# Building three small constant tables on chip instead of loading them, in a chunked state-space scan followed by a bilinear feed-forward layer

## The chip, the cores and the metric

The kernel runs on one core of a Trainium2 chip. The core has a matrix engine (TensorE, PE in the profile), a vector engine (VectorE, DVE), a scalar engine (ScalarE, ACT), a general engine (GpSimd, POOL) and a queue engine (SyncE, SP). Loads and stores are issued from the SP, ACT and POOL queues and are carried out by 16 DMA engines. The metric is the device time of one execution in microseconds (us), as a median of several runs; lower is better.

## The reference, cut to what matters

There are 4 batches, 8 heads, 768 tokens, head width D = 32 and state width N = 16. The first half is a chunked scan with a decaying state, the second a bilinear feed-forward layer on the 3072 x 256 result with 1536 hidden columns.

```python
for c in range(nc):                                   # chunks of the sequence
    cum = np.cumsum(la, axis=-1)                      # la: log of the decays a
    L = np.exp(cum[:, :, :, None] - cum[:, :, None, :]) * causal
    y_intra = np.einsum('bhij,bhjd->bhid', np.einsum('bhin,bhjn->bhij', Cc, Bc) * L, xc)
    y_inter = np.einsum('bhin,bhnd->bhid', Cc, state) * np.exp(cum)[:, :, :, None]
    y[:, :, sl] = y_intra + y_inter
    decay_full = np.exp(np.sum(la, axis=-1))
    Bx = np.einsum('bhjn,bhjd->bhjnd', Bc, xc) * np.exp(cum[:, :, -1:] - cum)[:, :, :, None, None]
    state = decay_full[:, :, None, None] * state + np.sum(Bx, axis=2)
# ... y of all heads side by side: x of 3072 x 256
out = (x @ w_a * (x @ w_b)) @ w_out
```

## The kernel before

The sequence is cut into NBLK = 6 blocks of Q = 128 tokens. Two batches of a block make a *pair* (p = 0 to 11), the unit of all loads of B, C and x (`load1`, `load2`). For each pair, `scale_bc` multiplies B and C by decay factors, `transposes` turns them for TensorE, `scores` forms C times B for each head, `mask(product(...))` multiplies the scores by a causal mask, and `pv` multiplies them by x and adds what the state of the block before gives. The result, X2T, goes through the feed-forward layer in units (`unit`, `unit_mm`): products with w_a and w_b, a copy of the first out of PSUM on ScalarE (`evac_a`), the product of the two on VectorE (`times`), and products with w_out (`out_mm`).

The order of work is written out by hand: each engine runs its instructions in the order of the program, so on each queue an instruction waits behind everything that stands ahead of it. Idle stretches of TensorE near the start are filled by `warmup` products of a tile of zeros, whose results are not used.

What matters here is the front of the program:

- SP's and ACT's queues issue a (the decays) and the B, C and x of pair 0. SP's also loads two constant tables: `ch` (128 x 10, line 188) and `c32` (32 x 148, line 194). `ch` holds `headm` (which head a row of a 128-row head-by-state tile belongs to) and `par` (whether that head is even or odd). `c32` holds `indm` (32 x 128, which head a column belongs to) and `selb` (which batch a row belongs to).
- GpSimd makes `sel` (32 x 32, a selector of batch and head, lines 197 and 198), then the identity `ident` (lines 207 and 208), then the mask `causal` (lines 211 and 214), and then issues seven loads: the rest of pair 1's B and C, the first halves of the weights Wa and Wb (`load_w(0)`, line 171), and pair 1's x in two halves (`xn`).
- VectorE clears `warm` and `zero`, waits for a and runs the decay products (`scan`, line 233); then `sel_over_mid` (line 239) forms `selr` out of `sel`, and `factors_mm` (line 254) turns decays into factors with small fp32 products.
- `ident` is used by `transposes`, `par` by the ACT copies in `transposes` (line 345) and by `state_spread` (line 596), and `headm` by `maskbd` (line 825).
- The decay of the state over a whole block, `hs` (32 rows of batch and head x 5 blocks), is needed on 128 rows of head and state as `G`. Before the change GpSimd first spreads `hs` to 32 x 20 (`hsx`, line 797), zero outside a row's own batch, and one fp32 product with `indm` gives all of `G` (line 815). ScalarE's queue then holds, in this order, the copy of the factors (`fC`, line 267), the copy of `G` (line 817) and the scaling of pair 1's x (`scale_x(1, nc.scalar)`, line 291), which `pv(1)` waits for (line 448).

Of the kernel before, what the change touches and what calls it, by code (L numbers as in the profile page):

```python
# [10 lines left out]
f32 = mybir.dt.float32  # L11
# [3 lines left out]
ALU = mybir.AluOpType  # L15
# [13 lines left out]
def kernel(  # L29
# [13 lines left out]
    nc = tc.nc  # L43

    nb, H, S, D = x.shape
    N = B.shape[-1]
# [6 lines left out]
    BH = nb * H  # L53
    NBP = nb // 2
    NP = NBP * NBLK
    NG = NBLK - 1
# [1 line left out]
    P2 = 6  # L58


    j = np.arange(128)
    bh = np.arange(BH)
    p32 = np.zeros((BH, 128 + nb * NG), np.float32)
    p32[:, 0:128] = (bh[:, None] % H) == (j[None, :] // N)
    for b in range(nb):
        p32[b * H : (b + 1) * H, 128 + b * NG : 128 + (b + 1) * NG] = 1.0
    p32_t = nc.inline_tensor(p32, "p32")
    ph = np.zeros((128, H + 2), np.float32)
    ph[:, 0:H] = (j[:, None] // N) == np.arange(H)[None, :]
    ph[:, H:] = (j[:, None] // N) % 2 == np.arange(2)[None, :]  # L70
    ph_t = nc.inline_tensor(ph, "ph")

    const = ctx.enter_context(tc.tile_pool(name="const", bufs=1))
    c32 = const.tile([BH, p32.shape[1]], f32, name="c32")
    ch = const.tile([128, H + 2], f32, name="ch")
    ident = const.tile([128, 128], f16, name="ident")
    causal = const.tile([128, 2, Q], f16, name="causal")
    sel = const.tile([BH, 2, NBP, H], f32, name="sel")
    indm = c32[:, 0:128]
    selb = c32[:, 128 : 128 + nb * NG]  # L80
    headm = ch[:, 0:H]
    par = ch[:, H:]

    big = ctx.enter_context(tc.tile_pool(name="big", bufs=1))
    a_sb = big.tile([BH, NBLK, Q], f32, name="a_sb")
# [22 lines left out]
    fCl = big.tile([128, NL, NBP * 2 * H], f32, name="fCl")  # L108
    hr = big.tile([BH, NG], f32, name="hr")
    hs = big.tile([BH, NG], f32, name="hs")  # L110
    hsx = big.tile([BH, nb, NG], f32, name="hsx")
    G = big.tile([128, nb, NG], f32, name="G")

    inp = ctx.enter_context(tc.tile_pool(name="inp", bufs=3))
# [31 lines left out]
    def load1(eng, p, which, bt, i0=0, n=64):  # L146
        blk, bp = divmod(p, NBP)
        if p >= P2:
            return eng.dma_start(
                by_token(pair_in[p][which])[:, bt],  # L150
                (B, C, x)[which][2 * bp + bt, :, blk * Q : (blk + 1) * Q, :].rearrange("h q n -> q h n"),
            )
        src = (B, C, x)[which][2 * bp + bt, :, blk * Q + 2 * i0 : blk * Q + 2 * i0 + 2 * n, :]
        return eng.dma_start(  # L154
            pair_in[p][which][64 * bt + i0 : 64 * bt + i0 + n].rearrange("i h r n -> i h (r n)"),
            src.rearrange("h (i r) n -> i h (r n)", r=2),
        )
# [24 lines left out]
    for p_ in range(3):  # L182
# [2 lines left out]
    load1(nc.sync, 0, 0, 0)  # L185
    load1(nc.scalar, 0, 1, 1)
    load1(nc.sync, 0, 1, 0, 0, 32)
    nc.sync.dma_start(ch, ph_t.ap())
    load1(nc.scalar, 0, 1, 0, 32, 32)
    nc.scalar.preload_act_table_set("natural_log_exp_and_others")  # L190
    load1(nc.scalar, 0, 2, 1)
    load1(nc.sync, 0, 2, 0)
    load1(nc.sync, 1, 0, 0)
    nc.sync.dma_start(c32, p32_t.ap())
    nc.vector.memset(warm.bitcast(u32), 0)
    nc.vector.memset(zero, 0.0)
    nc.gpsimd.memset(sel, 1.0)
    nc.gpsimd.affine_select(
        out=sel,
        in_=sel,  # L200
        compare_op=ALU.is_equal,
        fill=0.0,
        base=0,
        pattern=[[-H, 2], [-2 * H, NBP], [-1, H]],
        channel_multiplier=1,
    )
    nc.gpsimd.memset(ident, 1.0)
    nc.gpsimd.affine_select(
        out=ident, in_=ident, compare_op=ALU.is_equal, fill=0.0, base=0, pattern=[[-1, 128]], channel_multiplier=1
    )  # L210
    nc.gpsimd.memset(causal, 1.0)
    for bt in range(2):
        v = causal[64 * bt : 64 * bt + 64]
        nc.gpsimd.affine_select(  # L214
            out=v, in_=v, compare_op=ALU.is_ge, fill=0.0, base=0, pattern=[[-1, 2], [1, Q]], channel_multiplier=-2
# [49 lines left out]
    def factors(lo, hi, fps):  # L265
        factors_mm(lo, hi, fps)
        nc.scalar.copy(flat(fC, lo, hi), fps[:, 0 : (hi - lo) * 2 * NBP * H])
# [56 lines left out]
    def transposes(p, ps=None, between=None, apart=False):  # L324
        s = st[p]
        if ps is None:
            ps = [SC[0], SC[1]] if apart else None
            on_dve = apart
        else:
            on_dve = True  # L330
        TB, TC = (TT[:, 0:256], TT[:, 256:512]) if ps is None else [t_.bitcast(f16)[:, 0:256] for t_ in ps]
        for T_, src in ((TB, s["bm"]), (TC, s["cm"])):
            for r in range(2):
                nc.tensor.transpose(
                    T_[:, r * 128 : (r + 1) * 128], src[:, r].rearrange("p h n -> p (h n)"), ident
                )
            if between:
                between()
                between = None
        BT = mid.tile([128, 2, 2, 2, 64], f16, name="bt", tag="bt")  # L340
        CT = mid.tile([128, 2, Q], f16, name="ct", tag="ct")
        b_ = []
        for e in range(2):
            o_ = BT[:, e].rearrange("p r t i -> p (r t i)")
            b_.append(nc.scalar.activation(out=o_, in_=TB, func=AF.Copy, scale=par[:, e : e + 1]))
        c_ = (nc.vector.tensor_copy if on_dve else nc.scalar.copy)(
            CT.rearrange("p t (i r) -> p r (t i)", r=2), TC.rearrange("p (r c) -> p r c", r=2)
        )
        if apart:
            for i_ in b_:  # L350
                tc.declare_no_dep(c_.ins, i_.ins.name, reason="reads of two banks")
        s["BT"], s["CT"] = BT, CT
# [288 lines left out]
    def unit(p, k2, between=None):  # L641
        a_ps = unit_mm(p, k2, Wa)
        if between:
            between()
        b_ps = unit_mm(p, k2, Wb)
        asb = evac_a(a_ps)
        return lambda: times(p, k2, b_ps, asb)
# [138 lines left out]
    for bt in range(2):  # L786
# [7 lines left out]
    sel_over_mid(1, P2 // NBP, nc.vector)  # L794
    nc.gpsimd.tensor_tensor(out=hr, in0=Pr[:, 0:NG, Q - 1], in1=rmid[:, 0:NG], op=ALU.mult)
    nc.gpsimd.tensor_tensor(out=hs, in0=hr, in1=Pr[:, 1:NBLK, 63], op=ALU.mult)
    nc.gpsimd.tensor_tensor(
        out=hsx,
        in0=hs.unsqueeze(1).broadcast_to((BH, nb, NG)),
        in1=selb.rearrange("p (b g) -> p b g", b=nb),  # L800
        op=ALU.mult,
    )
    for bt in range(2):
        load1(nc.gpsimd, 2, 0, bt)
    warmup(2, tcp)
# [6 lines left out]
    asb.append(evac_a(aps[2]))  # L812
    fps = bank("fps")
    gps = fps[:, 96 : 96 + nb * NG]
    nc.tensor.matmul(gps, indm, hsx.rearrange("p b g -> p (b g)"), start=True, stop=True, skip_group_check=True)
    factors(1, P2 // NBP, fps)
    nc.scalar.copy(G.rearrange("p b g -> p (b g)"), gps)
    scale_x(1, nc.scalar)
# [36 lines left out]
    h = unit(1, 5)  # L855
# [20 lines left out]
    h = unit(2, 0, lambda: transposes(3, apart=True))  # L876
# [3 lines left out]
    h = unit(2, 1)  # L880
# [55 lines left out]
    for m in range(1, 4):  # L936
# [36 lines left out]
        out=causal_q, in_=causal_q, compare_op=ALU.is_ge, fill=0.0, base=0, pattern=[[1, Q]], channel_multiplier=-1  # L973
# [97 lines left out]
```

## Time and profile before

| what | before |
|---|---|
| device time, median of 3 runs | 125.04 us |
| device time, lowest and highest | 124.65 and 125.16 us |
| span of the profiled execution, first to last instruction | 123.5 us |
| TensorE / VectorE / ScalarE / GpSimd busy | 95% / 70% / 58% / 51% |
| granted TensorE clock | full speed throughout |
| packets that the DMA engines moved | 60754, 13.74 MB |

The span is what the trace can explain; the median of the runs lies 1.5 us above it, which is what lies around the first and the last instruction. Busy shares are averages over the whole span. A line of a timeline reads: start in us from the span's start, length in us, engine, line of the kernel, operation, what is written and read, how many, and in square brackets how long the engine had been idle and what ended that. The ends of matrix products are modelled: two of them that follow each other overlap in the rows, and the distance of their starts is what the engine spends on one.

### The profile page before, as it was taken

Reading aid. Unit: us, or ns where it says so; the run is one execution under the profiler, and the core shown is the slowest. Engines: PE = TensorE matmul, PEld = TensorE weight load, DVE = VectorE, ACT = ScalarE, POOL = GpSimd, SP = SyncE. Lnnn points to the kernel's source line nnn. Section 1 sums busy time; section 2 is a strip of 40 time slices with the busy share of each in tenths; the row PEclk is TensorE's granted clock in tenths of the full one; section 3 lists DMA queues with packets and bytes.
Section 4 is the critical chain, followed back from the end, with each engine's and each line's share of the span. In section 5 each row is a group of like instructions: output and inputs, shape, how many; then the busy total and the mean of one; then the engine's idle time right before and its main releaser. Section 6 shows DMA issues by size and latency. Waiting matters only on the chain.

```text
span 123.5 us, 3874 instructions
## 1 busy us (share of the span) xinstructions
PE 117.6 (95%) x1527; PEld 79.8 (65%) x1527; DVE 86.4 (70%) x166; ACT 71.9 (58%) x142; POOL 62.8 (51%) x109
## 2 busy tenths in 40 slices
PE   5988999999999999899999999999999999999990
PEld 2445698978898788644467455756464784655880
DVE  1886889795968979298984989857899444847100
ACT  0465845866364795687758746664737736566220
POOL 7999999956873399089850895026900000000000
PEclk9999999999999999999999999999999999999999
DMA  3999999994659988697995973999541012010132
GB/s 64 154 163 237 171 196 181 194 145 74 99 115 185 92 83 147 84 120 79 134 155 74 150 264 87 70 95 161 113 130 42 5 42 85 0 42 0 48 101 69
DMA packets 60754, 13.74 MB, mean 111 GB/s; under 512 B 55632, under 2 KB 60400, under 8 KB 60736
## 3 DMA queue, kind: packets, MB, share of 16 engines
q1 hardware_dynamic: 56608, 9.53, 49.8%
q0 software_dynamic: 2128, 3.61, 16.3%
q10 hardware_dynamic: 2000, 0.36, 1.6%
q8 instruction: 12, 0.20, 0.7%
q14 instruction: 6, 0.05, 0.1%
HBM read 11.13 MB, written 3.15 MB: 116 GB/s over the span
## 4 chain that ended last, share of the span: by engine, by line
PE 83%; DMA 6%; POOL 5%; ACT 2%; issue 1%; DVE 1%; ACTq 0%; POOLq 0%
PE ops L709 18%; PE aps L682 17%; PE bps L682 17%; PE ops L652 9%; PE aps L616 8%; PE bps L616 7%; DMA xn<-in_x_dram 6%; PE SC L373 2%; PE SC L448 1%; PE SC L433 1%; PE SC L388 1%; POOL cn L154 1%; PE SC L523 1%; PE SC L475 1%; POOL bn L154 1%; POOL causal L214 1%
## 5 line engine op out<-in xcount | busy, mean ns | idle before, releaser
L630 ACT COPY asb<-aps 128x512 f32<-128x512 f32 x72 | 41.9, 587 | 14.8 <-PE aps L682 9.7
L694 DVE TENSOR_TENSOR hkb<-bps,asb 128x512 f16<-128x512 f32 x48 | 32.3, 689 | 12.9 <-ACT asb L630 11.7
L682 PE MATMUL aps<-XB,Wa 128*128 128x512 f16 x96 | 28.6, 379 | 0.0
L682 PE MATMUL bps<-XB,Wb 128*128 128x512 f16 x96 | 28.5, 379 | 0.0
L709 PE MATMUL ops<-Wo,hkb 128*128 128x256 f16 (+1 forms) x204 | 22.5, 267 | 0.0
L709 PEld LDWEIGHTS <-hkb 128*128 128x128 f16 x204 | 18.5, 98 | 3.1
L637 DVE TENSOR_TENSOR hk<-bps,asb 128x512 f16<-128x512 f32 x24 | 16.2, 688 | 2.9 <-ACT asb L630 2.4
L682 PEld LDWEIGHTS <-Wb 128*128 128x128 f16 x96 | 9.9, 103 | 11.0 <-issue 0.2
L427 DVE TENSOR_TENSOR t<-SC,causal_q 128x512 f16<-128x512 f32 x21 | 13.4, 682 | 3.9 <-PE SC L373 3.9
L682 PEld LDWEIGHTS <-Wa 128*128 128x128 f16 x96 | 9.7, 103 | 9.1 <-issue 0.4
L616 PE MATMUL aps<-X2T,Wa 128*128 128x256 f16 x96 | 14.3, 273 | 0.4 <-DMA Wa<-in_moe_w_a_dram 0.3
L721 ACT ACTIVATE osb<-ops 128x256 f32<-128x256 f32 (+1 forms) x16 | 6.0, 377 | 14.3 <-PE ops L709 14.2
L616 PE MATMUL bps<-X2T,Wb 128*128 128x256 f16 x96 | 14.3, 273 | 0.0
L652 PE MATMUL ops<-Wo,hk 128*128 128x256 f16 x96 | 11.6, 273 | 0.0
L616 PEld LDWEIGHTS <-Wa 128*128 128x128 f16 x96 | 9.5, 103 | 2.0 <-DMA Wa<-in_moe_w_a_dram 0.8
L616 PEld LDWEIGHTS <-Wb 128*128 128x128 f16 x96 | 9.7, 103 | 0.7
L652 PEld LDWEIGHTS <-hk 128*128 128x128 f16 x96 | 8.9, 98 | 1.5 <-DVE hk L637 0.2
L293 POOL TENSOR_SCALAR x<-xn 128x512 f16<-128x512 f32 x6 | 9.0, 1493 | 1.7 <-DMA xn<-in_x_dram 1.3
L427 DVE TENSOR_TENSOR t<-SC,causal 128x512 f16<-128x512 f32 x13 | 8.2, 684 | 1.4 <-PE SC L388 1.3
L304 POOL TENSOR_TENSOR planes<-cn,fCl 128x256 f16<-128x256 f32 x6 | 3.7, 622 | 8.1 <-DMA cn<-in_C_dram 8.1
L425 POOL TENSOR_TENSOR t<-tmp,causal_q 128x512 f16<-128x512 f32 x3 | 3.5, 1159 | 7.3 <-ACT tmp L424 7.2
L553 ACT ACTIVATE XB<-SC 64x512 f16<-64x512 f32 (+1 forms) x9 | 5.3, 594 | 2.9 <-PE SC L462 1.6
(102 smaller groups left out, 128.8 us busy)
## 6 DMA issues: line engine op xcount, KB each, us to landing
out_dram<-osb SPq DMA_DIRECT2D x19, 128.0 KB, 1.8
xn<-in_x_dram SPq DMA_DIRECT2D x5, 256.0 KB, 5.3
xn<-in_x_dram SPq DMA_DIRECT2D x7, 128.0 KB, 3.4
Wa<-in_moe_w_a_dram POOLq DMA_DIRECT2D x2, 384.0 KB, 6.2
Wb<-in_moe_w_b_dram POOLq DMA_DIRECT2D x2, 384.0 KB, 7.8
Wo<-in_moe_w_out_dram POOLq DMA_DIRECT2D x2, 384.0 KB, 6.8
cn<-in_C_dram SPq DMA_DIRECT2D x6, 128.0 KB, 4.2
bn<-in_B_dram SPq DMA_DIRECT2D x6, 128.0 KB, 4.3
```

Source lines behind the costliest of these rows:

```text
L293: eng.tensor_scalar(xo, xi, XS, None, ALU.mult)
L304: eng.tensor_tensor(out=planes[p % 2][:, 4:6].rearrange("p t (h n) -> p t h n", n=N), in0=raw, in1=f.unsqueeze(3).broadcast_to((128, 2, H, ...
L427: nc.vector.tensor_tensor(out=o_, in0=i_, in1=c_, op=ALU.mult)
L553: nc.scalar.activation(out=XB[to, blk - P0 // NBP, :, bt].rearrange("p u j q -> p u (j q)"), in_=SCt[bt][fr, :, 0 : NBP * Q], func=AF.Copy ...
L616: nc.tensor.matmul(ps[:, kk * 2 * Q : (kk + 1) * 2 * Q], W[k // 6][:, f, k % 6 // 3 * 384 : (k % 6 // 3 + 1) * 384].rearrange("p (c kk) -> ...
L630: (nc.vector.tensor_copy if on_dve else nc.scalar.copy)(asb, a_ps)
L637: nc.vector.tensor_tensor(out=s["hk"][:, 2 * k2 : 2 * k2 + 2, :].rearrange("p k q -> p (k q)"), in0=b_ps, in1=asb, op=ALU.mult)
L652: nc.tensor.matmul(o_ps[:, 0:d_model], hk[:, k, bt * Q : (bt + 1) * Q], Wo[:, k, :], start=(k == 0), stop=(k == NK - 1), skip_group_check= ...
L682: nc.tensor.matmul(t_, W[k // 6][:, f, k % 6 // 3 * 384 : (k % 6 // 3 + 1) * 384].rearrange("p (c kk) -> p kk c", kk=3)[:, k % 3], XB[:, b ...
L694: return lambda: nc.vector.tensor_tensor(out=s["hk"][:, k], in0=ps[1], in1=asb, op=ALU.mult)
L709: nc.tensor.matmul(o_ps[:, 0:w], hk[:, k, c * Q : (c + 1) * Q], Wo[:, k, cs], start=(k == 0), stop=(k == NK - 1), skip_group_check=True,)
L721: nc.scalar.activation(out=o_sb[:, 0:w], in_=o_ps[:, 0:w], func=AF.Copy, scale=1.0 / (YS * YS))
```

## The change

The tables `ch` and `c32` and their two loads go. VectorE makes `sel`, `headm`, `par` and a new table `spread` (32 x 32 x 16) from the identity, between its two clears and its first scan: two copies and two sums. GpSimd no longer makes `sel`, and starts with the identity. `hsx` goes as well: `G` comes out of four products, one for each batch, whose weights are the part of `spread` that holds that batch's eight heads, and whose moving tile is `hs` itself. The order of all other instructions on all engines stays as it was.

```diff
-    j = np.arange(128)
-    bh = np.arange(BH)
-    p32 = np.zeros((BH, 128 + nb * NG), np.float32)
-    p32[:, 0:128] = (bh[:, None] % H) == (j[None, :] // N)
...
-    ph_t = nc.inline_tensor(ph, "ph")
...
-    c32 = const.tile([BH, p32.shape[1]], f32, name="c32")
-    ch = const.tile([128, H + 2], f32, name="ch")
+    headm = const.tile([128, H], f32, name="headm")
+    par = const.tile([128, 2], f32, name="par")
...
+    spread = const.tile([BH, BH, N], f32, name="spread")
...
-    nc.sync.dma_start(ch, ph_t.ap())
...
-    nc.sync.dma_start(c32, p32_t.ap())
     nc.vector.memset(warm.bitcast(u32), 0)
     nc.vector.memset(zero, 0.0)
-    nc.gpsimd.memset(sel, 1.0)
-    nc.gpsimd.affine_select(
-        out=sel,
...
     nc.gpsimd.memset(ident, 1.0)
     nc.gpsimd.affine_select(
         out=ident, in_=ident, compare_op=ALU.is_equal, fill=0.0, base=0, pattern=[[-1, 128]], channel_multiplier=1
     )
+    nc.vector.tensor_copy(
+        sel.rearrange("p t b h -> p b t h"),
+        ident[0:BH, 0:BH].rearrange("p (b t h) -> p b t h", b=NBP, t=2),
+    )
+    nc.vector.tensor_reduce(
+        headm, ident.rearrange("p (h n) -> p h n", n=N), axis=mybir.AxisListType.X, op=ALU.add
+    )
+    nc.vector.tensor_reduce(
+        par, headm.rearrange("p (m e) -> p e m", e=2), axis=mybir.AxisListType.X, op=ALU.add
+    )
+    nc.vector.tensor_copy(spread, ident[0:BH, 0:BH].unsqueeze(2).broadcast_to((BH, BH, N)))
...
-    nc.gpsimd.tensor_tensor(
-        out=hsx,
-        in0=hs.unsqueeze(1).broadcast_to((BH, nb, NG)),
-        in1=selb.rearrange("p (b g) -> p b g", b=nb),
-        op=ALU.mult,
-    )
...
     gps = fps[:, 96 : 96 + nb * NG]
-    nc.tensor.matmul(gps, indm, hsx.rearrange("p b g -> p (b g)"), start=True, stop=True, skip_group_check=True)
+    for b in range(nb):
+        nc.tensor.matmul(
+            gps[:, b * NG : (b + 1) * NG],
+            spread[:, b * H : (b + 1) * H].rearrange("p h n -> p (h n)"),
+            hs,
+            start=True,
+            stop=True,
+            skip_group_check=True,
+        )
```

More of the change, by code (lines that the diff above doesn't have):

```diff
@@ L58 @@
     P2 = 6
-    j = np.arange(128)
-    bh = np.arange(BH)
-    p32 = np.zeros((BH, 128 + nb * NG), np.float32)
-    p32[:, 0:128] = (bh[:, None] % H) == (j[None, :] // N)
[L65 to L70, printed above, removed]
-    ph_t = nc.inline_tensor(ph, "ph")
     const = ctx.enter_context(tc.tile_pool(name="const", bufs=1))
-    c32 = const.tile([BH, p32.shape[1]], f32, name="c32")
-    ch = const.tile([128, H + 2], f32, name="ch")
+    headm = const.tile([128, H], f32, name="headm")
+    par = const.tile([128, 2], f32, name="par")
     ident = const.tile([128, 128], f16, name="ident")
@@ L78 @@
     sel = const.tile([BH, 2, NBP, H], f32, name="sel")
[L79 to L82, printed above, removed]
+    spread = const.tile([BH, BH, N], f32, name="spread")
     big = ctx.enter_context(tc.tile_pool(name="big", bufs=1))
@@ L110 @@
     hs = big.tile([BH, NG], f32, name="hs")
-    hsx = big.tile([BH, nb, NG], f32, name="hsx")
     G = big.tile([128, nb, NG], f32, name="G")
@@ L193 @@
     load1(nc.sync, 1, 0, 0)
-    nc.sync.dma_start(c32, p32_t.ap())
     nc.vector.memset(warm.bitcast(u32), 0)
     nc.vector.memset(zero, 0.0)
-    nc.gpsimd.memset(sel, 1.0)
-    nc.gpsimd.affine_select(
-        out=sel,
[L200 to L205, printed above, removed]
-    )
     nc.gpsimd.memset(ident, 1.0)
@@ L796 @@
     nc.gpsimd.tensor_tensor(out=hs, in0=hr, in1=Pr[:, 1:NBLK, 63], op=ALU.mult)
-    nc.gpsimd.tensor_tensor(
-        out=hsx,
-        in0=hs.unsqueeze(1).broadcast_to((BH, nb, NG)),
-        in1=selb.rearrange("p (b g) -> p b g", b=nb),
-        op=ALU.mult,
-    )
     for bt in range(2):
```

## The prediction

> **What bounds the kernel now.** I read the page first: engine shares and the chain that ended last.
>
> ```profile
> PE 117.6 (95%) x1527; PEld 79.8 (65%) x1527; DVE 86.4 (70%) x166; ACT 71.9 (58%) x142; POOL 62.8 (51%) x109
> ...
> PE 83%; DMA 6%; POOL 5%; ACT 2%; issue 1%; DVE 1%; ACTq 0%; POOLq 0%
> ```
>
> TensorE carries the chain. GpSimd and one DMA hold 11% of it, some 14 us, and the chain in order of time says where: all of it at the front.
>
> ```profile
> 0.79 0.12 POOL sel L197
> ...
> 0.98 0.25 POOL sel L198
> ...
> 2.94 0.84 POOL bn L154
> ...
> 6.60 0.65 POOL xn L154
> 7.25 7.34 DMA xn<-in_x_dram
> ...
> 14.67 0.64 ACT x L291
> ...
> 15.36 0.42 PE SC L448 x32
> ```
>
> GpSimd's table work and load issues run up to the load of pair 1's x, which lands at 14.59; ScalarE scales it and `pv(1)` starts at 15.36. After that the chain is TensorE almost without a break, so a shift of `pv(1)` is carried to the end. The case is decided by what sets 15.36. The timeline around it:
>
> ```profile
> 10.37 0.59 PE L226 MATMUL tc<-warm 128*128 128x512 f16 x2
> ...
> 11.23 0.78 PEld L616 LDWEIGHTS <-Wa 128*128 128x128 f16 x8 [0.76 <-DMA Wa<-in_moe_w_a_dram]
> ...
> 13.13 0.29 PEld L815 LDWEIGHTS fps<-hsx,c 32*128 32x128 f32 x2 [0.21 <-issue]
> 13.13 0.39 PE L815 MATMUL fps<-hsx,c 32*128 32x20 f32 x2
> ...
> 14.22 0.24 ACT L267 COPY fC<-fps 128x64 f32<-128x64 f32 x1
> 14.32 0.22 ACT L817 COPY G<-fps 128x20 f32<-128x20 f32 x1
> 14.67 0.63 ACT L291 ACTIVATE x<-xn 128x512 f16<-128x512 f32 x1
> ...
> 19.78 0.64 POOL L312 TENSOR_TENSOR bm<-bn,fB 128x256 f16<-128x256 f32 x1
> ```
>
> A second chain runs beside the first, and the chain of waits does not print it: Wa lands (11.23), TensorE goes on without idling to the product for G and the factors, ScalarE's copies wait for them, and `scale_x(1)` stands behind those copies. fC lasts 0.24 and G begins 0.14 before its end, so ScalarE could take the scaling at about 14.54 - 0.12 = 14.42. This chain has 0.25 us to spare against 14.67.
>
> The front, where the new work goes:
>
> ```profile
> 1.15 0.17 DVE L196 MEMSET zero<- 32x128 f32 x1
> ...
> 1.45 0.29 POOL L208 TENSOR_SCALAR_AFFINE_SELECT ident<-ident 128x128 f16<-128x128 f16 x1
> ...
> 3.06 0.41 DVE L233 TENSOR_TENSOR_SCAN Pr<-a_sb,zero 32x128 f32<-32x128 f32 x1 [1.74 <-DMA a_sb<-in_a_dram]
> ...
> 9.19 0.41 DVE L312 TENSOR_TENSOR cm<-cn,fC 128x256 f16<-128x256 f32 x1
> 9.23 0.85 POOL L312 TENSOR_TENSOR bm<-bn,fB 128x256 f16<-128x256 f32 x1
> ```
>
> VectorE sits idle for 1.74 us before its first scan, waiting for a. The busy table by half microseconds has the DMA share second from the end:
>
> ```profile
> 5.00:5.50 0.50, 0.50 (x3) 0.13 (x1) 0.47 (x2) 0.00 (x0) 0.50 (x2) 1.00 0.52 116
> 5.50:6.00 0.50, 0.38 (x5) 0.18 (x4) 0.44 (x2) 0.01 (x1) 0.50 (x2) 1.00 1.07 245
> ```
>
> The DMA engines are half free until 5.5 and, but for short dips, full after that.
>
> **The change part by part.** *GpSimd's two `sel` instructions go.* `sel` begins at 0.79 and the identity's clear at 1.19, so all that GpSimd does up to the issue of x moves up by 0.40 us: the identity is done at 1.34 instead of 1.74, the first load is issued at about 2.5 and not 2.9.
>
> *VectorE makes the tables.* Its four instructions wait for the identity, from about 1.40. The copy for `sel` is 32 elements deep: 0.17, as the clear of `zero`. The sum over 128 elements lies between that 0.17 and the 0.42 of a product over 256: 0.30. The sum for `par` waits for `headm` (0.10, as from `rmid` to `selr`) and costs 0.15, as the reciprocal of `rmid`. The copy for `spread` writes 512 elements: 0.27 (the clear of `warm`, 256 words) to 0.69 (a product over 512); I take 0.69. Sum 1.41, end 2.81, under the wait for a that ends at 3.06. So they cost nothing, with 0.25 us of cover; what they are late beyond it, the first scan and all of pair 0 are late. `selr`, the next reader, comes at 3.76.
>
> *Two loads leave SP's queue.* The load of `ch` takes SP 0.49 us (2.70 to the next issue at 3.19), that of `c32` 0.33. Pair 0's x is issued 0.4 to 0.5 sooner, and pair 1's B after it. Worth nothing by itself: the scaling of pair 0's x (7.85) stands behind ScalarE's copy at 7.37. Nothing waited for these tables: `ch` landed 2.7 after its issue, at 5.4, and its first use begins at 5.99.
>
> *The loads land sooner.* With issues 0.40 sooner Wa lands at 10.83 in place of 11.23. TensorE is free at 10.79 (its two warm-up products begin 0.21 apart: 10.37 + 0.42). So 0.40 us gained for the second chain; bounds 0 (the DMA engines are full, the data come no sooner) and 0.44 (TensorE itself is late next). I take 0.40, because the half-free stretch up to 5.5 can take the sooner packets. x lands at 14.19.
>
> *`hsx` goes.* GpSimd gets 0.27 us (12.18 to 12.44), behind which stand pair 2's loads and a mask; neither is on the path. `hs` is ready at 12.10 and its product comes at 12.73 at the soonest, so the product does not wait.
>
> *Four products for one.* Each fp32 product is two passes (L815 x2), so two passes become eight. Two weight loads of 0.182 take 0.29 together, so a further pass costs 0.11, and the moving width, 20 before and 5 after, hardly matters beside that. Six passes more: 0.65 us on TensorE. Bounds: 0.35 (the factor products, half as wide, have a pair of passes each 0.058) and 1.09 (no overlap of loads at all). I take 0.65: it is the same shape. Nothing hides it: the factor products stand behind it, then fC, G and the scaling of x.
>
> *The sum.* The second chain moves by +0.65 - 0.40, less its 0.25 to spare: the scaling of x starts at 14.67 as before, `pv(1)` at 15.36. The long wait for x (ends at 14.19 now) becomes a wait for the copies of the factors. Net 0.00: span 123.5, and with the 1.5 us by which the median lies above that span, 125.0 us.
>
> **The rivals.** *The passes are cheap.* At the lower bound of 0.35 the scaling starts at 14.67 + 0.35 - 0.65 = 14.37, and the landed x allows 14.27. Gain 0.30, 124.7 us. For it: narrow products do run closer together. Against it: the weights are 128 wide as before.
>
> *The loads are issued sooner but land no sooner.* Then the change does not do what it says: the 0.40 is missing and `pv(1)` is 0.40 late, 125.4 us. For it: DMA shares at or over 1 from 5.5 on. Against it: 0.52 just before. The Trainium skill ("DMA: Bandwidth & Descriptors", section "Issuing engines are not separate DMA queues") says that loads from all queues interleave on the same 16 engines and that several issuers save only issue time; by that rule this rival's 125.4 would be the time. The trace agrees as far as the full shares go, not in the half-free stretch.
>
> *VectorE's copies and GpSimd get in each other's way.* GpSimd's `bm` took 0.85 at 9.23, beside a VectorE product with both inputs in SBUF, and 0.64 at 19.78. If the copy for `spread` must wait until GpSimd's last select for `causal` ends (2.94 before, 2.54 now), it ends at 2.54 + 0.10 + 0.69 = 3.33. If in turn GpSimd's first load must wait for that, its issues are 0.44 later than before (3.33 against 2.89) in place of 0.40 sooner. Then Wa is 0.44 late and `pv(1)` 0.65 + 0.44 - 0.25 = 0.84: 125.9 us, slower by 0.7%. It decides the sign once GpSimd's first load is issued over 0.62 us later than at 2.5 (Wa is then 0.22 late, and 0.65 + 0.22 - 0.25 = 0.62). Against it: the copy may run in 0.3, and it may find a gap. The Trainium skill ("SBUF — State Buffer", section "Who interferes with whom") has such a rule: GpSimd and a VectorE copy in its two-port mode exclude each other for a whole instruction, sums never do; by it something between 125.4 and 125.9 would result. The stretch at 9.23 fits its further clause on VectorE instructions with two SBUF inputs; no VectorE copy out of SBUF is in the front of this trace.
>
> **How the numbers follow.** The forecast (125.0, within 0.2 of it by an uncertain 0.2 in the landing of Wa): 0.52. Cheap passes, 124.7: 0.14. No sooner landing, 125.4: 0.18. The mutual block, 125.9: 0.11. Unseen: 0.05. The range 124.5 to 125.6 takes in the first three, with 0.2 at the lower end for the scatter of the runs (124.65 to 125.16) and 0.2 at the upper. Half a per cent, 0.62 us, is about what a measurement of this kernel can tell from no change. Faster by more than that needs 0.3 more than the cheap passes give, and the landing of x allows 0.40 at most (14.27 against 14.67): 0.05, the unseen. Slower by more: the block and a little of the third case, 0.12. Within: 0.83.
>
> **What would show it.** Right: identity done near 1.34; VectorE's tables done before 3.06 and the first scan there still; Wa's wait over near 10.8; eight passes on the four products (line 793 of the changed kernel) 0.11 apart, 0.9 us in all; the scaling of x waiting for TensorE's factors and no longer for the DMA; `pv(1)` within 0.2 of 15.36. Wrong: a first scan after 3.1, a first GpSimd load after 2.7, Wa after 11.0, or passes spaced by 0.06.

## The result and the profile after

The changed kernel takes 125.53 us (median of 22 runs, 124.63 to 126.46) beside 125.01 us for the kernel before (22 runs, 124.46 to 125.97): ratio 1.0048, 95% interval 1.0029 to 1.0067. By the ratio it is 0.6 us slower, 0.36 to 0.84 by the interval, where no change was forecast; the time itself lies inside the stated range of 124.5 to 125.6. Ratios leave out executions more than 1.5% above the fastest of their kernel, while the time printed beside a ratio is the median of all executions. The profiled execution took 125.46 us with a span of 123.8 (before: 125.04 and 123.5).

The page after, engine line and chain shares, and then the chain of waits in order of time:

```profile
PE 118.0 (95%) x1533; PEld 80.4 (65%) x1533; DVE 87.4 (71%) x170; ACT 71.7 (58%) x142; POOL 62.2 (50%) x106
...
PE 85%; POOL 6%; DMA 5%; ACT 1%; DVE 1%; issue 0%; POOLq 0%
```

```profile
4.83 6.09 DMA Wa<-in_moe_w_a_dram
...
10.96 1.06 PE aps L599 x8
...
12.93 0.98 PE fps L793 x8
13.91 0.58 PE fps L237 x16
14.50 0.99 PE bps L599 x8
15.48 0.35 PE SC L431 x32
```

TensorE executes six instructions more (1533 for 1527). The first wait of the chain is now for Wa and not for pair 1's x, and from 10.96 on TensorE goes without idling through the units of Wa, the eight passes of the four products (L793), the factor products (L237) and two units of Wb to `pv(1)` at 15.4. That is the second chain of the prediction, and it has become the first.

The front, from the timeline (start, duration, engine, line, operation, and idle time before with its releaser):

```profile
1.39 0.26 DVE L183 CAST sel<-ident 32x32 f32<-32x32 f16 x1
1.49 0.27 DVE L187 TENSOR_REDUCE headm<-ident 128x8 f32<-128x128 f16 x1
...
1.86 0.51 DVE L193 CAST spread<-ident 32x512 f32<-32x512 f16 x1
...
2.59 0.89 POOL L138 DMA_DIRECT2D bn<-in_B_dram  x1
2.85 0.41 DVE L216 TENSOR_TENSOR_SCAN Pr<-a_sb,zero 32x128 f32<-32x128 f32 x1 [0.47 <-DMA a_sb<-in_a_dram]
```

VectorE's tables are done at 2.37, and the first scan still waits for a: 0.47 us of its wait is left. GpSimd's first load starts at 2.59 where it was 2.89.

One pair of profiles says little here, since the landings differ by half a microsecond from run to run. So both kernels were profiled a second time. The timeline of the second profile of before:

```profile
10.77 1.05 PE L616 MATMUL aps<-X2T,Wa 128*128 128x256 f16 x8
...
12.66 0.39 PE L815 MATMUL fps<-hsx,c 32*128 32x20 f32 x2
...
12.99 0.66 PE L254 MATMUL fps<-selr,Pr 32*64 32x16 f32 x16
...
14.11 0.63 ACT L291 ACTIVATE x<-xn 128x512 f16<-128x512 f32 x1
...
14.80 0.55 PE L448 MATMUL SC<-t,x 64*32 64x128 f16 x32 [0.17 <-ACT x L291]
```

The timeline of the second profile of after:

```profile
10.74 1.04 PE L599 MATMUL aps<-X2T,Wa 128*128 128x256 f16 x8
...
12.62 1.05 PE L793 MATMUL fps<-hs,spread 32*128 32x5 f32 x8
...
13.60 0.66 PE L237 MATMUL fps<-selr,Pr 32*64 32x16 f32 x16
...
14.48 0.65 ACT L274 ACTIVATE x<-xn 128x512 f16<-128x512 f32 x1
...
15.18 0.42 PE L431 MATMUL SC<-t,x 64*32 64x128 f16 x32
```

Both start the units of Wa at the same time and come to the product at the same time. The factors then follow 0.33 us later before and 0.98 later after. The scaling of x is 0.37 late, `pv(1)` 0.38. In the first pair the same 0.65 was there, but Wa had landed late in before (its units began at 11.23), and `pv(1)` looked 0.06 late only. That the units begin together in the second pair is chance; what the two pairs share is the stretch from those units on.

### The profile page after: what moved, and what is told of

Its sections match the earlier page's. It is cut to its first block, busy times and chain, and to the rows that moved or that the text cites. A ratio compares the mean times of both kernels' runs of the same rounds, so it can differ in the third digit from the quotient of the medians.

```text
span 123.8 us, 3881 instructions
## 1 busy us (share of the span) xinstructions
PE 118.0 (95%) x1533; PEld 80.4 (65%) x1533; DVE 87.4 (71%) x170; ACT 71.7 (58%) x142; POOL 62.2 (50%) x106
## 4 chain that ended last, share of the span: by engine, by line
PE 85%; POOL 6%; DMA 5%; ACT 1%; DVE 1%; issue 0%; POOLq 0%
PE ops L692 17%; PE aps L665 17%; PE bps L665 17%; PE ops L635 9%; PE aps L599 8%; PE bps L599 7%; DMA Wa<-in_moe_w_a_dram 5%; POOL t L408 2%; PE SC L356 2%; PE SC L371 1%; PE SC L416 1%; POOL cn L138 1%; PE SC L431 1%; PE fps L793 1%; POOL causal L197 1%; PE SC L458 1%
## 6 DMA issues: line engine op xcount, KB each, us to landing
out_dram<-osb SPq DMA_DIRECT2D x19, 128.0 KB, 1.8
xn<-in_x_dram SPq DMA_DIRECT2D x7, 128.0 KB, 4.2
cn<-in_C_dram SPq DMA_DIRECT2D x6, 128.0 KB, 4.1
bn<-in_B_dram SPq DMA_DIRECT2D x6, 128.0 KB, 3.9
```

## The experiments

Two theories went in. P: the six added fp32 passes on TensorE are the loss, and nothing else in the change gives anything back. B: VectorE's table copies and GpSimd's selects get in each other's way. Later came M and L, on stalls near 48 us. Ratios are to the kernel before, run beside each kernel.

**The passes alone.** The kernel before, with its product issued four times:

```diff
-    nc.tensor.matmul(gps, indm, hsx.rearrange("p b g -> p (b g)"), start=True, ...)
+    for _ in range(4):
+        nc.tensor.matmul(gps, indm, hsx.rearrange("p b g -> p (b g)"), start=True, ...)
```

> The kernel before, with its one product for G issued four times (the same result each time): six passes more and nothing else. Theory P (the passes are the loss): the product group takes 0.9 us instead of 0.3, pv(1) starts 0.65 - 0.25 = 0.40 later than before, so +0.4 us, ratio about 1.003. Theory B (VectorE's tables and GpSimd block each other, and that is the loss): the passes hide in the wait for x, within 0.1 us of before.

Measured: 125.78 us, ratio 1.0026 (0.9989 to 1.0063). The profiled execution ran at a granted clock of 0.858, so its times say nothing. Run again:

> The kernel before with its one product for G issued four times (the same columns, the last result kept), so with the six added fp32 passes and nothing else of the change; the profile of its first run had a throttled clock and could not be compared. Theory P and the prediction's sum agree on it: 0.65 us more on TensorE, of which ScalarE's 0.25 of slack absorbs part, so pv(1) 0.4 us late and the time 0.4 us up if the shift is carried to the end, ratio 1.003. Theory M adds: with hsx in place pair 2's loads go out at 12.4, so the second Wb half lands by 18.8 and bm of pair 6 starts by 44.0; no stall at 48 in this kernel.

Measured: 125.49 us, ratio 1.0057 (1.0021 to 1.0093); `pv(1)` at 15.56. The passes alone cost 0.3 and 0.7 us, about what the changed kernel lost, though the first interval takes in no change. Theory M's part failed: `hsx` is in place here, and still the second Wb half landed at 19.05 and `bm` of pair 6 began at 45.08.

**The passes doubled.**

```diff
-    for b in range(nb):
+    for b in [*range(nb), *range(nb)]:
```

> The changed kernel with its four products issued twice, the same columns written again: sixteen fp32 passes in place of eight, and nothing else. Theory P (the added passes are paid in full, since nothing stands beside them any more): 8 x 0.108 = 0.86 us more on TensorE than the changed kernel, and 0.6 to 0.9 us more time; ratio to before 1.009 to 1.012. Theory S (the changed kernel's loss comes from stalls in the middle that move about, and the passes are absorbed): 0 to 0.3 us more than the changed kernel, ratio 1.003 to 1.007.

Measured: 126.51 us (6 runs), ratio 1.0139 (1.0089 to 1.0188). Three of the six executions, at a granted clock near 0.986, took 126.9 to 128.0 and lift the ratio; the other three took 126.0 to 126.1, 1.1 to 1.2 us over the 124.9 of before beside them. With the sixteen passes the factor products start 1.87 us after the first product, with eight 0.98, with two 0.32: 0.11 us for each further pass. Fourteen added passes make 1.55 us on TensorE. The three executions near full clock are 0.5 to 0.8 us above what the changed kernel lost (0.46 to 0.60): less than the 0.86 of the passes in full, and more than the 0.3 that theory S allows. So more passes cost more time; with three executions, by how much is only rough.

**The products made cheap.**

```diff
-    spread = const.tile([BH, BH, N], f32, name="spread")
+    spread = const.tile([BH, BH, N], bf16, name="spread")
-    hs = big.tile([BH, NG], f32, name="hs")
+    hs = big.tile([BH, NG], bf16, name="hs")
```

> The changed kernel with the table spread and the tile hs in bf16, so that each of the four products is one pass with a faster weight load: the group takes about 0.25 us instead of 1.0. Theory P: as with one product, 0.1 to 0.4 us faster than before. Theory B: 0.3 to 0.6 us slower than before, as the changed kernel.

Measured: 124.79 us, ratio 0.9984 (0.9943 to 1.0026). Run again:

> The changed kernel with spread and hs in bfloat16, one pass for each product (the decays of the states are rounded to 8 bits there), once more, beside the doubled products: the other end of the dose. Theory P: four cheap passes in place of eight, 0.5 us or more below the changed kernel, ratio 0.996 to 1.001. Theory S: as the changed kernel, 1.003 to 1.005.

Measured: 125.27 us, ratio 1.0034 (1.0007 to 1.0060). The four bfloat16 products take 0.18 us together, less than the two fp32 passes of before (0.32), and `pv(1)` starts at 15.04 and 14.77. The two ratios do not agree well, and the second lies in the range of theory S. Together they are 0.1% above before, about 0.4 us below the changed kernel. As a gain over before it is not shown.

**The tables alone.** One product with `hsx` as before, its 148-column table loaded; `sel`, `headm` and `par` made by VectorE, while `spread`, the largest table, is left out with the four products that used it:

```diff
-    nc.vector.tensor_copy(spread, ident[0:BH, 0:BH].unsqueeze(2)...)
+    nc.sync.dma_start(c32, p32_t.ap())
...
+    nc.gpsimd.tensor_tensor(out=hsx, in0=hs..., in1=selb..., op=ALU.mult)
-    for b in range(nb):
-        nc.tensor.matmul(gps[:, b * NG : (b + 1) * NG], spread[...], hs, ...)
+    nc.tensor.matmul(gps, indm, hsx..., ...)
```

> The changed kernel with its four products taken out: one product for G as before, with hsx on GpSimd and the table of 148 columns for it loaded by SP as before. VectorE still makes sel, headm and par from the identity, and the load of the 10 columns stays gone. Theory P (the six added fp32 passes are the loss, the tables are free): the product and the factors take TensorE no longer than before, pv(1) starts 0.1 to 0.3 us sooner than before, bounded by the GpSimd mask of pair 1 that ended near 15.1 with one product; 124.7 to 125.0 us, 0.1 to 0.3 us faster than before. Theory B (VectorE's copies beside GpSimd's selects are the loss): slower than before by 0.3 us or more, like the changed kernel. A third reading, that the one-product kernel was slow because its two tables for the product were made on chip: this kernel, which loads them, is then not slow, and the one-product kernel beside it is.

Measured: 125.05 us, ratio 0.9996 (0.9964 to 1.0027). In microseconds the interval is -0.45 to +0.34: little room is left for the 0.3 or more that B expected, and it is too wide to tell the 0.1 to 0.3 of gain that P expected from none. A version of it with the product's own tables also made by VectorE (two sums and a copy in place of the load):

> The changed kernel with one product for G again: VectorE makes the two parts of the old second table (32 x 128 and 32 x 4) from the identity too, and GpSimd forms the 32 x 20 tile again. All other parts of the change stay. Theory P: the loss goes and the sooner landing of Wa is left over, bounded by the landing of x: 0.1 to 0.3 us faster than before, scaling of x near 14.4. Theory B: the loss stays, 0.3 to 0.6 us slower than before.

Measured: 126.83 us, ratio 1.0054 (1.0005 to 1.0102); by the medians of all executions it is 1.4% over before. Once more:

> The kernel with one product and all tables made by VectorE once more, to see with a second profile where its longer executions (126.6 to 127.4 us against 125.0 to 125.5) lose their time. Theory P alone gives no reason for them and expects 124.7 to 125.0 us. A second theory, late landings: with the loads closer together at the start, pair 0's x lands late (at 8.1 in the first profile) and the first products start late in some executions. A third, stalls in the middle: the front is as in the first profile and a stall of 1 us or more stands at 45 to 70 us.

Measured: 126.78 us (6 runs), ratio 1.0110 (1.0035 to 1.0184). Most executions take 126.6 to 127.7 and some 125.0 to 125.8, and both profiled ones were of the second kind. Their front was as in the other kernels (`pv(1)` at 14.68 and 15.07), and TensorE waited 0.66 and 0.40 us near 67 us for the transposed planes of pair 9. That points to the third theory of the expectation, with shorter stalls than the 1 us it named; the long executions themselves were not profiled, so where they lose their time is not shown. The gain that P expected of this kernel is missed.

**GpSimd's head start taken away.** The changed kernel, with GpSimd building an unused table of the size of `sel` first:

```diff
+    nc.gpsimd.memset(dummy, 1.0)
+    nc.gpsimd.affine_select(out=dummy, in_=dummy, compare_op=ALU.is_equal, ...)
     nc.gpsimd.memset(ident, 1.0)
```

> The changed kernel with GpSimd made to build an unused 32 x 32 table first, as long as the old sel: its identity and its loads begin 0.40 later again, the rest of the change stays. Theory P with a head start that is worth 0.3 us: Wa lands near 11.2 and the time is 0.3 us above the changed kernel, +0.8 us over before. If the loads land no sooner for being issued sooner (DMA engines full): as the changed kernel, +0.5 us over before. Theory B: less than the changed kernel, since the tables fall beside other GpSimd work.

Measured: 125.22 us, ratio 1.0001 (0.9973 to 1.0030). Wa, issued at 5.22 and not at 4.83, landed at 10.45, sooner than in the changed kernel's first profile (10.92). Again:

> The changed kernel with GpSimd building an unused small table first, so that its identity and loads come 0.40 us later, once more: its first ratio was 1.0001 and not the changed kernel's 1.0037 to 1.0048. If GpSimd's head start costs time by itself (the loads collide), the ratio is again below 1.002. If the head start is worth nothing and the first run was scatter, the ratio is 1.003 to 1.006. If the head start is worth the prediction's 0.40 us, it is 1.006 or more.

Measured: 125.18 us, ratio 1.0015 (0.9992 to 1.0039); Wa landed at 10.85. Without the head start the kernel is not slower; if anything, faster. That is against P as well: this kernel has the six added passes, and neither ratio shows it slower than before. The cheap products with `sel` back on GpSimd, so also without the head start:

```diff
+    nc.gpsimd.memset(sel, 1.0)
+    nc.gpsimd.affine_select(out=sel, in_=sel, compare_op=ALU.is_equal, ...)
     nc.gpsimd.memset(ident, 1.0)
...
-    nc.vector.tensor_copy(sel.rearrange("p t b h -> p b t h"), ident[0:BH, 0:BH]...)
```

> The four products with spread and hs in bfloat16 (so one pass each and not two; the decays of the states are rounded to 8 bits there), and sel made by GpSimd again as before, so that GpSimd has no head start. Theory P, with the head start worth nothing: the same as the bfloat16 kernel with the head start, 124.5 to 124.9 us, ratio to before 0.996 to 1.000. If the head start is worth the 0.27 to 0.40 us of the prediction: 0.3 us slower than the bfloat16 kernel, ratio about 1.000 to 1.002.

Measured: 125.34 us, ratio 1.0010 (0.9967 to 1.0053). No difference to the bfloat16 kernel with the head start can be told.

**Both kernels once more, unaltered.**

> The changed kernel once more, unaltered, for a second profile and a second ratio. Theory P: ratio 1.003 to 1.007; products and factors 0.6 to 0.7 us longer on TensorE than before, and the wait for Wa over at a different place than 10.96, since the run without GpSimd's head start had Wa land at 10.45: if Wa's landing is scatter of the run, this profile can have it anywhere from 10.4 to 11.2. If the head start sets it, it is within 0.1 of 10.96 again. If the stall of about 0.7 us at 48 us, behind GpSimd's masks of pair 6, belongs to the changed kernel, it is there again; if it is scatter, it need not be.

Measured: 125.48 us, ratio 1.0037 (1.0003 to 1.0071). The units of Wa start at 10.74 and not at 10.96.

> The kernel before, unaltered, for a second profile and for the ratio that no change gives. Both theories: ratio within 0.002 of 1. Theory M: bm of pair 6 on GpSimd starts at 43.4 to 44.0 and TensorE does not wait at 48; the stall of 0.55 us at 51.9 of the first profile, absent in every other profile so far, is either there again (then it belongs to the kernel) or not (then the first profile showed a late case, and the profiles' spans mislead by that much).

Measured: 124.97 us, ratio 0.9990 (0.9961 to 1.0018). Its stall at 51.9 is gone, and there is one of 0.37 at 48.38 in its place, with `bm` of pair 6 at 44.87: against M, stalls in the middle belong to both kernels.

**The middle of the kernel.** In both profiles of after, TensorE waits at 48.8 for GpSimd's masks of pair 5, which stand behind `bm` of pair 6. From the timeline of the first:

```profile
45.29 0.62 POOL L295 TENSOR_TENSOR bm<-bn,fBl 128x256 f16<-128x256 f32 x1 [0.75 <-PE aps L599]
...
46.45 2.27 POOL L408 TENSOR_TENSOR t<-tmp,causal_r 128x512 f16<-128x512 f32 x2
...
48.78 0.31 PE L431 MATMUL SC<-t,x 64*32 64x128 f16 x16 [0.34 <-POOL t L408]
```

Theory M blamed the missing `hsx`, with which pair 2's loads went out later. First, pair 2's B loads put behind the mask of pair 1:

```diff
-    for bt in range(2):
-        load1(nc.gpsimd, 2, 0, bt)
     warmup(2, tcp)
...
     mask(product(1, 3), by_pool=True)
+    for bt in range(2):
+        load1(nc.gpsimd, 2, 0, bt)
```

> The changed kernel with GpSimd's two loads of pair 2's B issued behind its mask of pair 1 instead of ahead of it: the loads go out about 2 us later (14.3 in place of 12.1), and the mask no longer waits for their issue. Theory M: the second Wb half has the DMA engines to itself for longer and lands at 18.3 to 18.8, pair 3's loads start with it, no stall at 48; ratio 0.998 to 1.002. Theory P: as the changed kernel, 1.003 to 1.006, since the passes are still there.

Measured: 125.84 us, ratio 1.0053 (1.0023 to 1.0083). The second Wb half landed at 19.32, no sooner. `bm` of pair 6 began at 44.36 and TensorE did not wait at 48, yet the time is no better than the changed kernel's. M's forecast fails. Second, an idle product of `hsx`'s size behind `hs`:

```diff
+    nc.gpsimd.tensor_tensor(out=hsx, in0=hs.unsqueeze(1)..., in1=spread[:, 0:nb, 0:NG], op=ALU.mult)
     for bt in range(2):
         load1(nc.gpsimd, 2, 0, bt)
```

> The changed kernel with an idle GpSimd product of hsx's size put back where hsx was (its result is not read), so that GpSimd issues pair 2's two B loads at 12.4 as before and not at 12.07. Theory M (the loss is made in the middle: with hsx gone, pair 2's loads go out 0.37 us sooner, share the DMA engines with the second halves of Wa and Wb, and the second Wb half, for which pair 3's loads on SP wait, lands at 19.23 in place of 18.79; SP's loads run late from there, pair 6's B lands at 45.1 in place of 43.8, and GpSimd's masks of pair 5 behind it hold TensorE for 0.7 us at 48): the second Wb half lands by 18.8 again, bm of pair 6 starts by 44.0, no stall at 48, and the time is 0.3 to 0.6 us below the changed kernel's 125.5, ratio to before 0.999 to 1.002. Theory P (the six fp32 passes are the loss): ratio 1.003 to 1.006 as the changed kernel has.

Measured: 127.86 us (6 runs), ratio 1.0207 (1.0165 to 1.0250); the profiled execution had a granted clock of 0.661. For a profile at full clock:

> The changed kernel with the idle GpSimd product behind hs, once more, for a profile at full clock: its first time was 2% over before, 127.2 to 128.0 us, which neither theory P (125.5) nor theory M (125.0) gives. If the loss is at the front, pv(1) is 1.5 us or more late; if in the middle, the front is as in the changed kernel and stalls of 2 us in all stand behind 20 us, at a transfer or a GpSimd mask that can be named.

Measured: 128.15 us for the profiled execution. The front is that of the changed kernel (`pv(1)` at 15.38), and the loss stands at two places of the timeline, two waits:

```profile
49.68 0.31 PE L432 MATMUL SC<-t,x 64*32 64x128 f16 x16 [1.39 <-POOL t L409]
...
69.87 0.40 PE L357 MATMUL SC<-turned 32*128 32x128 f16 x16 [1.72 <-DMA turned<-planes]
```

So in this execution loads on SP, GpSimd's planes and masks, and SP's transposes form a second loop, which falls behind TensorE. Why 0.22 us of GpSimd at 12.3 costs 2 us there is not settled.

Last, theory L: that loop is what the changed kernel is slow by. Pair 3's loads wait by hand for the second half of Wb; let them wait for that of Wa, in both kernels:

```diff
-    tc.add_manual_dep(b3[0].ins, w1[1].ins.name, AFTER, ...)
+    tc.add_manual_dep(b3[0].ins, w1[0].ins.name, AFTER, ...)
```

> The changed kernel with one word altered: pair 3's loads on SP wait for the second half of Wa (landed at 17.3) and no longer for the second half of Wb (19.2). In the profiles so far the state product of pair 5 starts when both TensorE gets there and GpSimd's masks of pair 5 are done, which stand behind bm of pair 6; in the changed kernel the masks were last both times (done at 48.7, TensorE could have started at 47.5 to 47.8). Theory L (the loop of SP's loads and GpSimd's planes is the second chain, and it starts at that wait): SP's loads run up to 1.9 us sooner, bm of pair 6 starts by 44.0 in place of 45.3, no stall at 48, and the time is 0.3 to 0.7 us below the changed kernel, ratio 0.997 to 1.001. Theory P alone (the loop does not matter for the median): as the changed kernel, 1.003 to 1.006. If the second Wb half, now beside pair 3's loads, lands over 0.5 us later than 19.2, TensorE waits for it at 19.4 and the gain is eaten there.

Measured: 125.43 us, ratio 1.0060 (1.0027 to 1.0092).

> The kernel before with the same one word altered. Theory L: bm of pair 6 by 44.0 and no stall at 48; the masks were late in one profile of before and not in the other, so the gain is smaller, 0.1 to 0.4 us, ratio 0.997 to 0.999, and the six passes are seen undisturbed as the difference to the changed kernel with the same word altered: 0.3 to 0.5 us. Theory P alone: ratio 1.000, and the same difference.

Measured: 124.98 us, ratio 1.0003 (0.9978 to 1.0028). `bm` of pair 6 starts at 44.62 and 44.20, neither profile has a stall at 48, and neither time is better for it. By the ratios the difference between the two kernels stays as it was, and L fails: the wait at 48 alone does not make it. The difference is not one even shift either. With the moved wait, five of the changed kernel's twelve executions took 126.2 to 126.6 and the rest 124.8 to 125.7; ten of before's took 124.7 to 125.2 and two 125.8 and 125.9. The profiled one of the changed kernel took 124.81, so its profile can't show where the long ones lose their time.

No kernel here is shown faster than before.

## Why the prediction was wrong

**The six passes at 0.65 us.** Right. From the start of Wa's units to the factors it is 2.20 to 2.22 us in all profiles with two passes and 2.86 to 2.90 in all with eight at full clock: 0.66. The rival of cheap passes is out. (Its bound of 0.35 took the 0.06 us between two pairs of factor passes for the price of one pass.)

**The 0.40 us for Wa landing sooner.** This is the step that failed. First, GpSimd's head start was 0.30 and not 0.40: its second select for `causal` lasted 0.50 beside VectorE's copy for `spread`, where before it lasted 0.41. Second, the use of Wa follows the issue only loosely. In seven profiles with the issue at 5.1 to 5.2, Wa's units start on average at 11.02 (10.77 to 11.40); in eleven with the issue at 4.75 to 4.84, at 10.94 (10.60 to 11.32). That is 0.09 us for an issue 0.35 sooner, far inside the scatter of one kernel: before had 11.23 and 10.77. The changed kernel with its head start taken away agrees: 10.81 and 10.89 without it, 10.96 and 10.74 with it. Third, where Wa does land early nothing is won, since TensorE's own warm-up products end near 10.74: after had Wa at 10.32 in its second profile and started at 10.74. The prediction named that limit, as 10.79, but took its room below it from the one profile it had, in which Wa landed late.

The reason that the prediction gave for taking 0.40 was misread too. It called the DMA engines half free until 5.5 and showed the row from 5.0 on. The rows just ahead of that one, in the same table of before (DMA share second from the end), say otherwise:

```profile
4.00:4.50 0.50, 0.50 (x10) 0.37 (x8) 0.50 (x2) 0.25 (x1) 0.50 (x2) 1.00 0.93 133
4.50:5.00 0.50, 0.50 (x7) 0.26 (x6) 0.31 (x2) 0.00 (x0) 0.50 (x1) 1.00 1.38 150
```

A row counts packets by their start, so its share can exceed 1. Wa's issue moved from 5.13 to 4.83, into the half microsecond that had 1.38 before the change, and not into a stretch that was half free.

**ScalarE's 0.25 us of slack.** About right. From the start of Wa's units to `pv(1)` it is 4.12, 4.03 and 4.10 in the profiles of before and of before with the moved wait, 4.43 to 4.47 in all full-clock profiles with eight passes. So 0.37 of the 0.65 arrive and 0.28 are absorbed. Worked out as the prediction did it (the scaling could begin 0.12 before the copy of G ends), the slack is 0.25, 0.16 and 0.24 in these three profiles.

**The sum.** With the measured head start it is 0.65 - 0.25 - 0.09 = 0.31 late at `pv(1)`, and not 0.00. That is near the rival of loads that land no sooner, whose price was 125.4 us; measured were 125.53 and 125.48. Its reason holds in part only. Over the same two groups of profiles Wa itself landed 0.18 sooner (10.74 on average for 10.93, each group spread over 0.9 us or more), which can't be told from nothing, but the second half of pair 1's x landed 0.66 sooner (13.67 for 14.33). The prediction cited a rule of the Trainium skill for this rival ("DMA: Bandwidth & Descriptors", section "Issuing engines are not separate DMA queues"), that issuing from several engines saves only issue time: Wa's landing agrees with it, and that of x does not show it. The sooner x is of no use in the changed kernel, whose scaling waits for the factors. The 0.31 lies inside the interval of the second ratio (0.04 to 0.89 us) and just below that of the first (0.36 to 0.84); the rest is not explained.

**Carried to the end.** Not shown. In the second pair `pv(1)` is 0.38 late and TensorE is level at 19.4, where before waits 0.18 for the second Wb half. Ahead of the masks at 48 after is 0.09 late (the state product of pair 5 starts at 47.25 and 47.16), behind them 0.41, and 0.42 at its last product: most of this lateness was made at 48, where after waited 0.69 and before 0.37. In the first pair `pv(1)` is 0.06 late and the last product 0.13; with the moved wait `pv(1)` of the changed kernel is 0.47 sooner and its last product 0.12 sooner. So the front of three pairs of single executions does not give the loss of the medians. Between 20 and 70 us each execution has its own stalls, which swallow a shift or pass it on.

**The tables under the wait for a.** Right, with more room than forecast: they took less than the 1.41 us summed, above all the copy for `spread` (0.51 for 0.69), and the first scan came 0.21 us sooner than before, because a did. **The mutual block** did not happen: first load at 2.59, first scan at 2.85, and the tables alone, without `spread`, are at ratio 0.9996. Of `spread` the front shows the 0.09 us by which it lengthened GpSimd's last select.

**Open.** That the passes are on TensorE and cost it 0.66 us there is shown; that they alone make the loss is not. For it: the passes alone lose about as much, and more of them lose more. Against it: the changed kernel without the head start is at 1.0001 and 1.0015, with it at 1.0048 and 1.0037, and the passes are in both. By the front the head start is worth 0.09 us; by these ratios it costs some 0.4. The kernels with one product and all tables on chip, and with the idle product, are 1 to 2% longer, with their profiled stalls in the loop of GpSimd and SP. Both suggest that small shifts on GpSimd's side of the front decide which stalls come later; which shift leads to which stall was not found.

## What to carry to other kernels

On an engine that is 95% busy, expect to pay for an added pass: price it by the row of its own shape, and count what pays it back only if it is shown in the same units. A gain that rests on a transfer landing sooner needs two things read from more than one profile: how much that landing scatters by itself, and when the engine that waits for it would be free anyway. A claim that the transfer engines have room needs the rows on both sides of the one that shows it. Where the whole claim is half a per cent, profile the old kernel twice before subtracting.

## What the runs showed of the hardware

- A 32-row fp32 product with 128 columns of weights takes two passes, and each further pass cost 0.11 us (16 passes in 1.87 us, 8 in 0.98, 2 in 0.32), whether 5 or 20 columns moved (8 passes in 0.98 and 0.99). Four of the same shape in bfloat16 took 0.18 us together, 0.045 each.
- The same load in the same kernel landed at 11.19 and 10.72 (before), at 10.92 and 10.32 (after), and, in the changed kernel with its issue 0.4 us later, at 10.45 and 10.85.
- Pair 1's x, issued some 0.35 us sooner, landed 0.66 us sooner on average (seven and eleven profiles); Wa, ahead of it in the same queue, 0.18.
- Small VectorE table work in this front: a 32x32 copy 0.26 us, a sum of 128x128 to 128x8 0.27, one to 128x2 0.16, a 32x512 copy from f16 to f32 0.51.
